# Seven block products for the gate projection of the last two token tiles

## The chip, the cores and the metric

The kernel runs on one core of a Trainium2 chip. The core has four engines that matter here and a queue engine. TensorE (PE) multiplies matrices into eight PSUM banks. VectorE (DVE) and ScalarE (ACT) can read PSUM and SBUF. GpSimd (POOL) reads and writes SBUF only. SyncE (SP) issues DMAs, and POOL issues DMAs as well. Each engine takes its instructions in the order in which they were written; an instruction that waits holds up everything behind it on its engine. The metric is the device time of one execution in microseconds (us).

## What is computed

A causal attention over 8 batches, 8 heads, 576 positions and a head size of 64, whose scores get a bias made of a running sum of `s`, is followed by a gated feed-forward block over its 4608 x 512 output `x`:

```python
g = x @ w_gate                                # 512 -> 1536
silu = g * (1.0 / (1.0 + np.exp(-g)))
val = x @ w_val                               # 512 -> 1536
out = (silu * val) @ w_out                    # 1536 -> 512
```

The change touches only the first two of these lines, and only for the last 1024 of the 4608 tokens.

## The kernel before, in words

**Tiles.** The feed-forward block goes over nine tiles of 512 tokens (`TT`, `NTT`), numbered 0 to 8. For a tile, `xt` is the transposed attention output: 128 partitions x 4 channel blocks x 512 tokens, bf16, in the ring `XT`. The 1536 inner features are twelve blocks of 128 (`ft`), taken in six pairs. `ffn_items(tt)` is the tile's work: `gate_value` (24 items), then `down_plain` (tiles 0 and 1) or `down_seven` (from tile 2, `FIRST7`). The main loop at the end takes these items one by one. After each it may issue a helper (loads, casts), and then `pump` issues as much attention work of later heads as is due. Attention lasts until tile 6; tiles 7 and 8 hold feed-forward work alone.

**Gate and value.** For each block `ft`, four matmuls of 512 columns make the gate product in a bank (L650, `wg`). ACT writes tanh(g/2) (L671, `th`). DVE makes (th + 1) * g (L673, `pp`). Four more matmuls make the value product (L650, `wv`), and DVE multiplies the two with a factor 0.5 (L684), which gives the block of `ht`. So silu comes out of tanh, whose table holds exp as well.

**Down projection.** `down_seven` already computes the product with `w_out` from seven block products instead of eight (Strassen's scheme). For that it needs, for each pair, sums of the `ht` blocks (`su`, two DVE instructions, L691 and L692) and differences that overwrite two blocks of `ht` (L693, on POOL, except the last pair's, which DVE makes). Its matmuls have 256 columns (L756). Its first 20 matmuls take the products of pairs 0 to 4 (`m3`, `m4`); then those of pair 5 follow; then `m1`, `m6`, `m5`, `m2`, `m7`. Between them ACT copies results from PSUM (L871 `s`, L805 `ysb`), DVE adds (L873, L795 into `de`; L815 into `ysb`), and POOL subtracts (L821). `m7` adds to a bank half that L795 has to have read first. POOL issues the stores of `ysb` (L828); in the last tile SP does.

**Banks.** `take()` hands out the PSUM bank that was given back longest ago, in the order of the code. A product that gets a bank waits until the last reader of its earlier contents has finished.

**Around it.** POOL also masks the attention weights (L388, L393), issues the DMAs of the attention output `xs` (L444), which SP transposes into `XT` (L451), and the small `kq` DMAs (L188). DVE copies transposed keys and queries (L288). `raw` holds loaded keys and queries, `KQ` their transposed forms, `VT` the values.

## Time and profile before

Three runs gave 373.15, 373.44 and 373.95 us, a median of 373.44 us. The profiled execution took 373.17 us, with a span of 371.5 us from its first to its last instruction.

| | busy us | share of the span |
|---|---|---|
| PE, matmuls | 361.1 | 97% |
| DVE | 289.9 | 78% |
| ACT | 241.2 | 65% |
| POOL | 219.6 | 59% |

| stage | first product at us | down projection from us | ends at us |
|---|---|---|---|
| tile 6 | 272.3 | 298.4 | 307.5 |
| tile 7 | 307.5 | 328.2 | 337.5 |
| tile 8 | 337.5 | 358.1 | 367 |

A profile row gives the line, the engine, the operation, the tile written and the tile read with their shapes, a count, the busy time and mean, and then the time that the engine was idle before such instructions and what ended it. Matmuls overlap in the records: a row says 379 ns for one of 512 columns, while the next starts about 216 ns later, so the pace of PE is read from start to start. In the timeline, instructions of a kind that follow each other are one line with the start of the first.

### The profile page before, as it was taken

How to read it: one execution, taken by the hardware profiler on the slowest of the kernel's cores; microseconds unless marked ns; L12 is line 12 of the kernel's file. 1: busy time of each engine (PE TensorE's matmuls, PEld its weight loads, DVE VectorE, ACT ScalarE, POOL GpSimd, SP SyncE). 2: the span in 40 equal slices, each digit the busy share in tenths (PEclk: the TensorE clock that was granted, in tenths of full speed). 3: DMA queues.
4: the chain of work that ended last, by engine and by line, in shares of the span. 5: the costliest groups of instructions: out<-in, count | busy, mean ns of one | idle time of the engine just before them, and what ended most of it. 6: DMA issues, size and time to landing. Idle time of an engine off the chain costs nothing.

```text
span 371.5 us, 8742 instructions
## 1 busy us (share of the span) xinstructions
PE 361.1 (97%) x3248; PEld 230.2 (62%) x3288; DVE 289.9 (78%) x583; ACT 241.2 (65%) x472; POOL 219.6 (59%) x334
## 2 busy tenths in 40 slices
PE   7899999999999999999999999999999999999995
PEld 6675556555555557755685568555865585476464
DVE  8878786288985999589967987689768867975984
ACT  8879776778886976687858875786466423323321
POOL 8996795945366556694749465965575506315320
PEclk9999999999999999999999999999999999999999
DMA  7999999899898985995689575995161113002003
GB/s 237 218 269 282 202 282 274 235 332 188 251 231 244 255 197 166 206 317 177 181 187 256 160 188 171 233 185 157 40 144 39 35 35 113 0 2 102 14 0 113
DMA packets 92301, 64.21 MB, mean 173 GB/s; under 512 B 72620, under 2 KB 78116, under 8 KB 92260
## 3 DMA queue, kind: packets, MB, share of 16 engines
q1 hardware_dynamic: 79188, 37.92, 42.9%
q0 software_dynamic: 13072, 25.75, 26.5%
q8 instruction: 25, 0.41, 0.5%
q14 instruction: 16, 0.13, 0.1%
HBM read 37.90 MB, written 19.86 MB: 155 GB/s over the span
## 4 chain that ended last, share of the span: by engine, by line
PE 89%; POOL 4%; DVE 3%; ACT 1%; issue 1%; DVEq 0%; POOLq 0%
PE banks L650 47%; PE banks L756 17%; PE banks L373 10%; PE banks L410 8%; PE banks L707 5%; POOL rawv L162 1%; DVE kq L330 1%; PE banks L301 1%; DVE ht L684 1%; ACT pt L383 1%; DVE pp L673 1%; PE banks L459 1%; DVE kq L288 0%; POOL cq L260 0%; POOL ck L260 0%
## 5 line engine op out<-in xcount | busy, mean ns | idle before, releaser
L383 ACT ACTIVATE pt<-banks 128x512 bf16<-128x512 f32 (+1 forms) x256 | 120.6, 510 | 28.8 <-PE banks L373 16.6
L650 PE MATMUL banks<-XT,wg 128*128 128x512 bf16 x418 | 110.3, 379 | 0.7
L650 PE MATMUL banks<-XT,wv 128*128 128x512 bf16 x412 | 109.3, 379 | 1.1
L671 ACT ACTIVATE th<-banks 128x512 bf16<-128x512 f32 x108 | 64.7, 599 | 54.8 <-PE banks L650 51.8
L673 DVE SCALAR_TENSOR_TENSOR pp<-th,banks 128x512 bf16<-128x512 bf16 x108 | 73.7, 682 | 19.5 <-ACT th L671 19.0
L684 DVE SCALAR_TENSOR_TENSOR ht<-pp,banks 128x512 bf16<-128x512 bf16 x108 | 74.2, 687 | 10.6 <-DVE pp L673 0.5
L373 PE MATMUL banks<-kq 128*128 128x128 bf16 (+4 forms) x576 | 76.2, 240 | 0.5 <-DVE kq L288 0.3
L693 POOL TENSOR_TENSOR ht<-ht 128x512 bf16<-128x512 bf16 x35 | 40.4, 1154 | 52.8 <-DVE su L691 52.7
L373 PEld LDWEIGHTS <-kq 128*128 128x128 bf16 x576 | 46.0, 98 | 30.2 <-issue 2.0
L650 PEld LDWEIGHTS <-wv 128*128 128x128 bf16 x432 | 38.4, 98 | 36.1 <-issue 0.2
L650 PEld LDWEIGHTS <-wg 128*128 128x128 bf16 x432 | 38.3, 98 | 33.6
L410 PEld LDWEIGHTS <-pt 128*128 128x128 bf16 x960 | 41.8, 98 | 17.4 <-issue 0.2
L388 POOL TENSOR_SCALAR_AFFINE_SELECT pt<-pt 128x512 bf16<-128x512 bf16 x56 | 36.5, 652 | 25.5 <-ACT pt L383 22.8
L410 PE MATMUL banks<-vt,pt 128*128 128x65 bf16 x960 | 46.8, 194 | 0.1
L444 POOL DMA_DIRECT2D xs<-ot x24 | 21.7, 903 | 29.2 <-DVE ot L427 28.6
L756 PEld LDWEIGHTS <-ht 128*128 128x128 bf16 x336 | 31.2, 98 | 4.3
L427 DVE TENSOR_TENSOR ot<-banks,rc 128x320 bf16<-128x320 f32 x64 | 31.5, 492 | 2.2
L188 POOL DMA_DIRECT2D kq<-HL x48 | 29.2, 610 | 0.5 <-issue 0.4
L756 PEld LDWEIGHTS <-su 128*128 128x128 bf16 x252 | 23.6, 98 | 3.3
L707 PE MATMUL banks<-wo,ht 128*128 128x512 bf16 x90 | 24.8, 379 | 0.3
L821 POOL TENSOR_TENSOR ysb<-ysb 128x512 f32<-128x512 f32 x12 | 15.3, 1272 | 15.3 <-DVE ysb L815 15.3
L756 PE MATMUL banks<-WS,ht 128*128 128x256 bf16 x168 | 22.9, 273 | 0.0
(101 smaller groups left out, 385.0 us busy)
## 6 DMA issues: line engine op xcount, KB each, us to landing
out_dram<-ysb POOLq DMA_DIRECT2D x32, 256.0 KB, 3.7
rawv<-in_v_dram SPq DMA_DIRECT2D x24, 256.0 KB
rawk<-in_k_dram SPq DMA_DIRECT2D x10, 576.0 KB
rawq<-in_q_dram SPq DMA_DIRECT2D x10, 576.0 KB
xs<-ot POOLq DMA_DIRECT2D x24, 160.0 KB, 3.4
ks<-ck SPq DMA_DIRECT2D x11, 288.0 KB
qs<-cq SPq DMA_DIRECT2D x11, 288.0 KB
rawk<-in_k_dram POOLq DMA_DIRECT2D x5, 576.0 KB, 6.6
```

Source lines behind the costliest of these rows:

```text
L373: nc.tensor.matmul(sc[:, o : o + w], T[:, 1, e * S + 128 * tj : e * S + 128 * (tj + 1)], T[:, 0, e * S + lo : e * S + hi], start=not maske ...
L383: nc.scalar.activation(pt[:, c0 : c0 + n], sc, AF.Exp, scale=0.125)
L388: nc.gpsimd.affine_select(pt[:, 1088:1600], pt[:, 1088:1600], pattern=[[0, 4], [1, 128]], compare_op=ALU.is_ge, fill=zreg, base=0, channel ...
L410: nc.tensor.matmul(av[:, bi * (D + 1) : (bi + 1) * (D + 1)], pt[:, c0 : c0 + 128], VT[b % 2][:, tj, h, :], start=(tj == 0), stop=(tj == bi),)
L427: nc.vector.tensor_mul(ot[:, :, e * D : (e + 1) * D], av3[:, :, 0:D], rc[:, :, None].to_broadcast([128, NCH, D]),)
L650: nc.tensor.matmul(view(bs, TT), w[:, c, f0 : f0 + 128], xt[:, c, :], start=(c == 0), stop=(c == 3),)
L671: nc.scalar.activation(th, pg, AF.Tanh, scale=0.5)
L673: nc.vector.scalar_tensor_tensor(pp, in0=th, scalar=1.0, in1=pg, op0=ALU.add, op1=ALU.mult)
L684: nc.vector.scalar_tensor_tensor(hp[:, 2 * k2 : 2 * k2 + 2, :].rearrange("p a n -> p (a n)"), in0=pp, scalar=0.5, in1=pv, op0=ALU.mult, op ...
L693: (nc.vector if ft == NFT - 1 else nc.gpsimd).tensor_sub(hp[:, 1:3, :], hp[:, 1:4:2, :], hp[:, 0:3:2, :])
L707: nc.tensor.matmul(view(pys[ts_], DM), hps[ft // 2][:, 2 * (ft % 2) + half, c0 : c0 + 128], WO[j][:, ft % WKO, :], start=(ft == 0), stop=( ...
L756: nc.tensor.matmul(ps, lhs(p), rhs(p), start=(first and p == 0), stop=(last and p == NP - 1), skip_group_check=True,)
```

## The change

**Gate by seven products.** In tile 7 for four of the six pairs, and in tile 8 for five, the gate product of a pair is split into blocks: two halves of the channels (k), two feature blocks (h), two halves of the tokens (t). Strassen's scheme makes the four results from seven products of two matmuls each, 256 columns wide: 14 matmuls in place of 8 of 512 columns. It needs five sums of the weight blocks (`gate_sum`, ten POOL instructions, each 768 or 512 elements a partition, into buffers of `raw` that are no longer in use) and five sums of the token blocks for each tile (`x_sum`, DVE, into `VT`). The products land in two banks, `bx` and `by`. The results are put together in fp32 in SBUF, in the place of `KQ`.

**The steps of a pair.** They are letters in the word lists `GATE7`, followed by the pair's or block's number:

- `A` makes the products 3, 4 (into `bx`), 6, 1 (into `by`); ACT copies `bx` to `S2`; POOL adds its halves into `D3`.
- `M`: DVE adds product 1 to that sum.
- `B` makes products 5, 2 and 7; ACT copies `bx` (two finished results) to `G4`; POOL subtracts it from `D3` (512 elements, fp32); ACT applies Silu to the two finished results.
- `R`: DVE adds `by` to `D3`, which gives the other two results; ACT applies Silu to them.
- `G` is a plain gate block with Silu straight from PSUM; `V` a value product; `H` DVE's multiplication of a block; `U` the two sums and the difference of a finished pair; `X` a sum of token blocks.

The words are issued in the order of the list, each engine keeping its own part of it.

**Silu.** In these two tiles the ScalarE function is Silu, so the multiplication that followed tanh (L673) is gone. A Silu of one element in tile 6, after the last exp, brings its table in; no other table is loaded after it.

**Hooks and stores.** The weight sums are issued at items 8, 12, ... 32 of tile 5 and 4, 8, 12 of tile 6. Two token sums of tile 7 are issued in tile 6's down projection, and the five of tile 8 in tile 7's. The stores of tiles 6 and 7 are issued by SP, not POOL.

```diff
--- before.py
+++ after.py
@@ -696,6 +696,170 @@
                     sus.append(su)
                 yield 1.0
 
+        GATE7 = {
+            NTT - 2: (
+                "G0 V0 X1 X0 X4 H0 G1 A1 V1 H1 M1 A2 U0 B1 V2 M2 "
+                "A3 R1 M3 V3 H2 B2 V4 H3 A4 R2 U1 M4 V5 H4 B3 V6 H5 "
+                "G10 R3 U2 V7 H6 B4 V8 H7 G11 R4 U3 H8 V9 H9 V10 U4 H10 V11 H11 U5"
+            ),
+            NTT - 1: (
+                "A0 M0 V0 A1 M1 B0 V1 A2 R0 H0 M2 B1 V2 H1 "
+                "A3 R1 U0 M3 V3 H2 B2 V4 H3 A4 R2 U1 M4 V5 H4 B3 V6 H5 "
+                "G10 R3 U2 V7 H6 B4 V8 H7 G11 R4 U3 H8 V9 H9 V10 U4 H10 V11 H11 U5"
+            ),
+        }
+        QT = TT // 2
+        gsum = {}
+        kqf = [
+            [t.rearrange("p a n -> p (a n)").bitcast(FP32) for t in row] for row in KQ
+        ]
+        G4 = [kqf[0][i][:, 0:1024].rearrange("p (a n) -> p a n", a=4) for i in range(2)]
+        D3 = [
+            kqf[1][i // 2][:, i % 2 * 512 : i % 2 * 512 + 512].rearrange("p (a n) -> p a n", a=2)
+            for i in range(3)
+        ]
+        S2 = kqf[1][1][:, 512:1024].rearrange("p (a n) -> p a n", a=2)
+
+        def gate_sum(i, j):
+            if i not in gsum:
+                tag = "raw" + "kkkqq"[i]
+                rawg = raw.tile([128, NR, J, D], FP32, tag=tag, name=tag)
+                gsum[i] = rawg.rearrange("p r j d -> p (r j d)").bitcast(BF16)[
+                    :, 0:1536
+                ].rearrange("p (j c a f) -> p j c a f", j=2, c=2, a=3)
+            n = 3 - j
+            w = WG[j].rearrange("p (k c) (a h f) -> p k h c a f", k=2, a=3, h=2)
+            dst = gsum[i][:, j, :, 0:n, :]
+            (k0, h0), (k1, h1), op = (
+                ((0, 0), (1, 1), ALU.add), ((0, 1), (1, 1), ALU.add), ((0, 0), (1, 0), ALU.add),
+                ((0, 1), (0, 0), ALU.subtract), ((1, 0), (1, 1), ALU.subtract),
+            )[i]
+            nc.gpsimd.tensor_tensor(
+                dst, w[:, k0, h0, :, 0:n, :], w[:, k1, h1, :, 0:n, :], op
+            )
+
+        def x_quarter(tt, k, t):
+            xt = XT[:, :, (tt % 3) * TT : (tt % 3 + 1) * TT]
+            return xt[:, 2 * k : 2 * k + 2, t * QT : (t + 1) * QT]
+
+        def x_sums(tt):
+            t = VT[tt % 2].rearrange("p c h e -> p (c h e)")
+            return t[:, 0 : 10 * QT].rearrange("p (s c n) -> p s c n", s=5, c=2)
+
+        def x_sum(tt, i):
+            (k0, t0), (k1, t1), op = (
+                ((0, 0), (1, 1), ALU.add), ((0, 1), (1, 1), ALU.subtract),
+                ((1, 0), (0, 0), ALU.subtract), ((0, 0), (0, 1), ALU.add),
+                ((1, 0), (1, 1), ALU.add),
+            )[i]
+            nc.vector.tensor_tensor(
+                x_sums(tt)[:, i], x_quarter(tt, k0, t0), x_quarter(tt, k1, t1), op
+            )
+
+        def gate_value_seven(tt, hps, sus):
+            xt = XT[:, :, (tt % 3) * TT : (tt % 3 + 1) * TT]
+            xs = x_sums(tt)
+            bx, by, sg, vb = {}, {}, {}, {}
+
+            def m(i, p, ps, start, stop):
+                j, a = divmod(p, 3)
+                for c in range(2):
+                    if i in (3, 4):
+                        k = i - 3
+                        lhs = WG[j][:, 2 * k + c, (2 * a + k) * 128 : (2 * a + k + 1) * 128]
+                    else:
+                        lhs = gsum[{1: 0, 2: 1, 5: 2, 6: 3, 7: 4}[i]][:, j, c, a, :]
+                    if i in (2, 5):
+                        rhs = x_quarter(tt, i // 5, i // 5)[:, c, :]
+                    else:
+                        rhs = xs[:, {1: 0, 3: 1, 4: 2, 6: 3, 7: 4}[i], c, :]
+                    nc.tensor.matmul(
+                        ps, lhs, rhs, start=(start and c == 0), stop=(stop and c == 1),
+                        skip_group_check=True,
+                    )
+
+            def halves(b):
+                return view(b, TT)[:, 0:QT], view(b, TT)[:, QT:TT]
+
+            def both(b):
+                return view(b, TT).rearrange("p (a n) -> p a n", a=2)
+
+            def open_pair(p):
+                bx[p] = take()
+                by[p] = take()
+                m(3, p, halves(bx[p])[0], True, False)
+                m(4, p, halves(bx[p])[1], False, False)
+                m(6, p, halves(by[p])[1], True, True)
+                m(1, p, halves(by[p])[0], False, False)
+                nc.scalar.copy(S2, both(bx[p]))
+                nc.gpsimd.tensor_add(D3[p % 3][:, 0], S2[:, 0], S2[:, 1])
+
+            def middle(p):
+                d = D3[p % 3]
+                nc.vector.tensor_add(d[:, 1], d[:, 0], halves(by[p])[0])
+
+            def close_pair(p):
+                m(5, p, halves(bx[p])[0], False, True)
+                m(2, p, halves(bx[p])[1], False, True)
+                m(7, p, halves(by[p])[0], False, True)
+                g = G4[p % 2]
+                pt = PTP[0].tile([128, PTW], BF16, tag="pt", bufs=PTP["bufs"], name="pt")
+                sg[p] = pt[:, 0 : 4 * QT].rearrange("p (a n) -> p a n", a=4)
+                nc.scalar.copy(g[:, 1:3], both(bx[p]))
+                give(bx[p])
+                nc.gpsimd.tensor_sub(D3[p % 3], D3[p % 3], g[:, 1:3])
+                nc.scalar.activation(sg[p][:, 1:3], g[:, 1:3], AF.Silu)
+
+            def result(p):
+                g = G4[p % 2]
+                nc.vector.tensor_add(g[:, 0:4:3], D3[p % 3], both(by[p]))
+                give(by[p])
+                nc.scalar.activation(sg[p][:, 0:4:3], g[:, 0:4:3], AF.Silu)
+
+            def plain(ft):
+                bs = products("g", ft, xt)
+                pp = hpool.tile([128, TT], BF16, tag="pp", name="pp")
+                nc.scalar.activation(pp, view(bs, TT), AF.Silu)
+                give(bs)
+                p, h = divmod(ft, 2)
+                sg[p, h] = pp
+
+            def value(ft):
+                vb[ft] = products("v", ft, xt)
+
+            def times(ft):
+                p, h = divmod(ft, 2)
+                if h == 0:
+                    hps.append(hpool.tile([128, 4, HT], BF16, tag="ht", bufs=NP, name="ht"))
+                left = (
+                    sg[p, h] if (p, h) in sg
+                    else sg[p][:, 2 * h : 2 * h + 2].rearrange("p a n -> p (a n)")
+                )
+                nc.vector.tensor_mul(
+                    hps[p][:, 2 * h : 2 * h + 2, :].rearrange("p a n -> p (a n)"),
+                    left, view(vb[ft], TT),
+                )
+                give(vb.pop(ft))
+
+            def sums(p):
+                hp = hps[p]
+                su = PTP[0].tile([128, 3, HT], BF16, tag="su", bufs=NP, name="su")
+                nc.vector.tensor_add(su[:, 0:2, :], hp[:, 0:2, :], hp[:, 2:4, :])
+                nc.vector.tensor_add(su[:, 2, :], hp[:, 0, :], hp[:, 3, :])
+                (nc.vector if p == NP - 1 else nc.gpsimd).tensor_sub(
+                    hp[:, 1:3, :], hp[:, 1:4:2, :], hp[:, 0:3:2, :]
+                )
+                sus.append(su)
+
+            does = {
+                "A": open_pair, "M": middle, "B": close_pair, "R": result, "G": plain,
+                "V": value, "H": times, "U": sums, "X": lambda i: x_sum(tt, i),
+            }
+            for word in GATE7[tt].split():
+                does[word[0]](int(word[1:]))
+                if word[0] in "GVAB":
+                    yield 1.0
+
         def down_plain(tt, hps):
             pys = {}
 
@@ -823,7 +987,7 @@
                     )
                 flush()
 
-                def store(eng=nc.sync if end else nc.gpsimd):
+                def store(eng=nc.sync if tt >= NTT - 3 else nc.gpsimd):
                     for i in range(2):
                         eng.dma_start(
                             out[a + i * HT : a + i * HT + 128, :],
@@ -891,7 +1055,7 @@
         def ffn_items(tt):
             hps, sus = [], []
             flush()
-            yield from gate_value(tt, hps, sus)
+            yield from (gate_value_seven if tt in GATE7 else gate_value)(tt, hps, sus)
             if tt < FIRST7:
                 yield from down_plain(tt, hps)
             else:
@@ -1067,6 +1231,17 @@
         at_item(17, w_load, "o", 1)
         at_item(21, load_one, 5, "k", (0, NR), nc.gpsimd)
         at_item(23, load_one, 5, "q", (0, NR), nc.gpsimd)
+        at_tile = {}
+        for i in range(10):
+            key = (NTT - 4, 8 + 4 * i) if i < 7 else (NTT - 3, 4 * i - 24)
+            at_tile[key] = [lambda i=i: gate_sum(*divmod(i, 2))]
+        at_tile[NTT - 3, 26] = [
+            lambda: nc.scalar.activation(warm, warm, AF.Silu),
+            lambda: x_sum(NTT - 2, 2),
+        ]
+        at_tile[NTT - 3, 28] = [lambda: x_sum(NTT - 2, 3)]
+        for i in range(5):
+            at_tile[NTT - 2, 24 + i] = [lambda i=i: x_sum(NTT - 1, i)]
         for tt in range(NTT):
             lo = H * (tt + 1) + LAGS[tt]
             hi = min(H * (tt + 2) + LAGS[tt + 1], BH + 2)
@@ -1089,7 +1264,7 @@
                     do_later(1)
                 if seconds:
                     seconds.pop(0)()
-                for f in hook.pop(n, ()):
+                for f in hook.pop(n, ()) if tt == 0 else at_tile.get((tt, i), ()):
                     f()
                 done = min(1.0, max(0, n - n0) / (span - n0))
                 if tt == 0:
```

## The prediction

> **What bounds the kernel now.** I read the page first, then busy times by stage, then the rows of tile 7's gate stage by form, then timelines at the joints. Of the page, the engines and the chain that ended last:
>
> ```profile
> PE 361.1 (97%) x3248; PEld 230.2 (62%) x3288; DVE 289.9 (78%) x583; ACT 241.2 (65%) x472; POOL 219.6 (59%) x334
> ...
> PE 89%; POOL 4%; DVE 3%; ACT 1%; issue 1%; DVEq 0%; POOLq 0%
> ```
>
> PE is the bound. The gate stages of tiles 7 and 8 (each engine's busy us, then clock and DMA):
>
> ```profile
> 307.50:328.20 20.70, 20.59 (x96) 9.39 (x97) 17.98 (x33) 7.37 (x13) 9.56 (x11) 1.00 0.14 51
> 337.50:358.10 20.60, 20.49 (x95) 9.32 (x96) 17.99 (x33) 7.26 (x13) 9.78 (x11) 1.00 0.14 52
> ```
>
> PE never waits, DVE is nearly full, ACT and POOL have more than half free. The rows of tile 7's stage that give prices:
>
> ```profile
> L684 DVE SCALAR_TENSOR_TENSOR ht<-pp,banks 128x512 bf16<-128x512 bf16 x11 | 7.6, 688 | 1.3
> L673 DVE SCALAR_TENSOR_TENSOR pp<-th,banks 128x512 bf16<-128x512 bf16 x11 | 7.5, 682 | 1.0 <-ACT th L671 1.0
> L671 ACT ACTIVATE th<-banks 128x512 bf16<-128x512 f32 x12 | 7.2, 597 | 13.3 <-PE banks L650 12.2 <-DVE pp L673 1.1
> L693 POOL TENSOR_TENSOR ht<-ht 128x512 bf16<-128x512 bf16 x5 | 5.8, 1151 | 10.3 <-DVE su L691 10.3
> L821 POOL TENSOR_TENSOR ysb<-ysb 128x512 f32<-128x512 f32 x2 | 2.5, 1263 | 5.0 <-DVE ysb L815 5.0
> L691 DVE TENSOR_TENSOR su<-ht 128x512 bf16<-128x512 bf16 x5 | 2.1, 424 | 0.2
> L692 DVE TENSOR_TENSOR su<-ht 128x256 bf16<-128x256 bf16 x5 | 1.4, 285 | 0.0
> L815 DVE TENSOR_TENSOR ysb<-de,banks 128x512 f32<-128x512 f32 x1 | 0.7, 689 | 1.3 <-PE banks L756 1.3
> L805 ACT COPY ysb<-banks 128x512 f32<-128x512 f32 x1 | 0.6, 585 | 1.4 <-PE banks L756 1.4
> ```
>
> See that POOL is slow at elementwise work: 1.15 us for what DVE does in 0.42. And the timeline at tile 8's handover to the down projection:
>
> ```profile
> 358.14 2.78 PE L756 MATMUL banks<-wo,ht 128*128 128x256 bf16 x24
> ...
> 360.21 0.42 DVE L693 TENSOR_TENSOR ht<-ht 128x512 bf16<-128x512 bf16 x1
> ...
> 360.76 0.82 PE L756 MATMUL banks<-WS,su 128*128 128x256 bf16 x6
> ```
>
> DVE finishes the last pair 2.5 us after PE's last value product (358.14 to 360.63). The 24 matmuls of m3 and m4 cover exactly that; there is no further cover. From a tile's first gate product to m1 it is 23.34 us (307.53 to 330.87).
>
> **What PE saves.** Eight 512-column matmuls start 1.726 us apart (309.26 to 310.99); 84 of 256 columns take 9.17 us, 0.109 each, weight loads hidden. A pair falls from 1.726 to 14 x 0.109 = 1.529: 0.197 saved, and 1.77 us over nine pairs. That is the whole gain, and it stands only if nothing else holds PE.
>
> **What a pair costs elsewhere.**
> - DVE: the two L673 (1.36) go. M is 0.42 (as L795), R 0.69 (as L815), two H stay at 0.69. 3.45 becomes 3.19 with U.
> - ACT: two copies (0.585) and two Silu (0.60, as tanh; the trace has no Silu, and 512-element ACT rows of several functions lie at 0.59 to 0.60): 2.37 of 3.25 us. Not a bound.
> - POOL: one U difference before (1.15); now also the 256-element fp32 addition and the 512-element fp32 subtraction. The subtraction is L821's shape: 1.27; its lower bound is a one-input POOL operation of that width (L388, 0.65), and I take 1.27, since type and inputs agree. The addition lies between 0.24 (L393) and 1.27, taken as 0.70; it hides beside R. Together 3.12 us a pair, against PE's 3.25 (1.53 gate, 1.73 value).
>
> **The loop.** POOL is full, and it also waits. On POOL, `U1` stands between the subtractions of pairs 2 and 3; on DVE, `U1` stands behind `R2`, and `R2` waits for the subtraction of pair 2. So from one subtraction to the next: 1.27 + 0.10 (POOL to DVE; not shown, between ACT to DVE 0.04 and DVE to POOL 0.15) + 0.61 (R; an independent DVE instruction starts 0.08 before the recorded end) + 0.42 (U's first sum) + 0.15 (DVE to POOL, 306.51 to 306.66) + 1.09 (POOL's U, start to start) = 3.64 us. PE's pair takes 3.25. The other loop, through ACT (R, Silu, then the copy of the next pair), is 1.27 + 0.10 + 0.69 + 0.09 + 0.60 + 0.585 + 0.07 = 3.40: also longer.
>
> **Tile 7, written down queue by queue** (us from its first product, each instruction in code order at its row's time). Five pieces of G and V, and A1, A2 and B1 follow without a wait. POOL does the additions of pairs 1 and 2 (to 6.3), then U0 (to 7.5). The subtraction of pair 1 starts at 7.45, those of 2, 3, 4 at 10.86, 14.49, 18.12. R4 ends at 20.18. Behind it DVE has U3, H8, H9, U4, H10, H11: 3.87 us, to 24.05. PE by its own work would be through at 19.92 and at m1 at 22.55. Now m4 of pair 5 waits for H11, and m1 starts at 24.44: 1.10 later than the 23.34 of before. A bank wait of 0.65 at A4 (H2 still reads) lies inside that.
>
> **Tile 8.** It starts with a seven-product pair, and POOL's last L821 of tile 7 ends 2.35 us into it (as before: 309.88 - 307.53), ahead of the first addition. Subtractions start at 4.40, 7.81, 11.44, 15.07, 18.70. H11 ends at 24.6, m1 starts at 25.0: 1.66 late.
>
> **Other edits.**
> - Token sums: 0.42 each (L691). Tile 7's first three fit before A1's later products. Of tile 8's five, four stand ahead of L873 in tile 7's down projection, which begins late; L795 then ends about 28.6, m7 is due at 28.37: 0.25 us, bounds 0 and 0.7.
> - Weight sums on POOL: 1.15 (512) and 1.64 (768; scaled with the 0.18 that L388 and L393 leave as fixed). In tile 5 one of 1.15 comes behind the `kq` DMAs and ahead of the select at 262.35; that then ends 263.75, and PE's matmuls that need it were at 263.18: 0.65. The other selects have 0.6 to 2 us in hand. Bounds 0 and 2.0 (below).
> - The table load (L204, 1.28 us and 0.20 for the element): ACT idles 2.94 before L871 at 300.96. Nothing; without that cover 1.5.
> - Stores to SP: behind SP's last transpose (304.25) nothing waits; POOL sheds 2.18 us after 309.82. Nothing; were SP late, stores would still have a tile's time.
>
> One row speaks against the weight sums: DVE's copies of L288 next to POOL's selects.
>
> ```profile
> 246.29 0.46 DVE L288 COPY kq<-pk 64x1152 bf16<-64x1152 bf16 x1
> ...
> 263.52 0.93 DVE L288 COPY kq<-pk 64x1152 bf16<-64x1152 bf16 x1
> ```
> ```profile
> 263.47 0.65 POOL L388 TENSOR_SCALAR_AFFINE_SELECT pt<-pt 128x512 bf16<-128x512 bf16 x1
> ```
>
> The second copy lasted until POOL's instruction was over. Two copies (246.29 and 250.88) will meet a sum and may wait about 1.0 each; DVE idles 7.3 of the 39 us there, so I take nothing, with 2.0 as the upper end. The Trainium skill, "SBUF — State Buffer", section "SBUF: two separate sides", says that VectorE and GpSimd lock a shared port pair for whole instructions, when VectorE runs in a two-port mode or reads two SBUF inputs. By that rule every such copy waits out the sum, and the total would be up to 2.0 us above mine; by the rows of the uncrowded copies (0.46) it would be mine.
>
> **The sum**, on the profiled execution's 373.17 us (span 371.5 and 1.67 around it; 0.27 below the median): 373.17 + 0.65 + 1.10 + 0.25 + 1.66 = 376.83. PE's saving is inside the two tile terms.
>
> **The rivals.**
> - *POOL keeps up, and PE stays the bound* (faster). Place: the subtraction. It decides if the loop falls below 3.25, so if the subtraction takes 0.88 or less. For it: the lower bound of 0.65. Against it: L821 is the same type, shape and number of inputs. The last subtraction could then start when B4's copy is there (16.47 in tile 7, 16.27 in tile 8), and m1 would start at 22.79 and 22.59: 373.17 - 0.55 - 0.75 = 371.9, or 372.5 with the 0.65.
> - *Half way.* Waits and lags eat about the saving: 372.7 to 374.2.
> - *Longer lags.* Each hand-over 0.15, and no DVE instruction starts before the recorded end of the last: the loop is 3.81. The same list then gives m1 at 25.25 and 26.0 and 0.7 at m7: 373.17 + 0.65 + 1.9 + 0.7 + 2.7 = 379.1.
> - *The clock drops while PE waits.* PE's waits would add up to 1.9 and 2.7 us in the two tiles. Against it: around PE's wait of 0.64 us at 14.0 the granted clock read 1.00, as in every 5 us of the first 40; the trace has no longer wait between matmuls. If 3.4 us after each tile's wait ran at half speed, 1.7 a tile is added: 376.8 + 3.4 = 380.2. The Trainium skill, "TensorE: Matmul & The Clock Gate", section "What's actually happening", says that the array falls to half its clock after an idle window of about 3.4 us; by that rule waits as short as these don't do it.
>
> That the products pace slower than counted I exclude: the 0.109 is measured with fresh weights each time.
>
> **How the numbers follow.** Forecast (374.2 to 378.2) 0.60, longer lags 0.12, clock 0.03, half way 0.10, POOL keeps up 0.15. A measurement of this kernel tells apart about 0.2%, 0.75 us. Faster 0.15, same 0.10, slower 0.75. The predicted time is 376.8. The range leaves out the clock's case and most of the fast one: 372.6 to 379.2.
>
> **What would show it.** POOL over 85% busy in both gate stages, its subtraction near 1.27 us and 3.6 us from one to the next; R waiting for POOL; PE waits at m3, m4 or A for DVE's multiplications, about 1.9 us in tile 7 and 2.7 in tile 8 in all; products of A and B 0.109 apart; one wait near 263. I am wrong if the subtraction takes under 0.9 us, or if the tail from R4 to H11 is much shorter than 3.9 us.

## The result, and the profile after

The changed kernel took 381.90 us (median of six runs, 380.9 to 383.87), against 373.29 us before (six runs on the same chip): a ratio of 1.0228, with a 95% interval of 1.0204 to 1.0251. It is slower, as forecast, but by 8.6 us where 3.7 were forecast, and 2.7 us beyond the upper end of the range. The profiled execution took 383.87 us, with a span of 382.1.

The page of the changed kernel, engines and the chain that ended last:

```profile
PE 366.6 (96%) x3342; PEld 236.3 (62%) x3342; DVE 292.2 (76%) x587; ACT 252.4 (66%) x492; POOL 246.0 (64%) x354
...
PE 62%; DVE 14%; POOL 9%; DMA 6%; issue 5%; ACT 2%; DVEq 0%; POOLq 0%; ACTq 0%
```

PE's own work is not the story: it was 89% of the chain and is 62% now, and DVE, POOL and loads have taken the difference. To place the loss, I compare the starts of landmarks in the two traces: DVE's 64 instructions that write the attention output (L427 in both), and then the first `m1` matmul of tiles 6, 7 and 8.

| stretch | lag behind before at its end, us | added in it, us |
|---|---|---|
| start, and tiles 0 to 4 (code that is the same) | 2.73 | 2.73 |
| tile 5, gate stage | 4.52 | 1.79 |
| tile 5, handover to the down projection | 8.94 | 4.42 |
| tile 6 | 8.95 | 0.01 |
| `m1` of tile 6 to `m1` of tile 7 | 9.85 | 0.90 |
| `m1` of tile 7 to `m1` of tile 8 | 11.05 | 1.20 |

The first row is not the change's. In that execution some DMAs landed late, at the start and again between 89 and 119 us; all eleven kernels below run that code, and the profiles of nine show 0.0 to 0.3 there, those of two 2.6 and 3.1. It is a matter of single executions. (At the other end, from tile 8's `m1` to the end of the span, before takes 0.4 us more than the changed kernel.) What is left is 6.2 us in tile 5 and 2.1 us in tiles 7 and 8. The forecast had 0.65 and 3.0 for these two.

The line numbers shift with the code: in the changed kernel the weight sums are L737, the matmuls of the down projection L920 and those of the seven products L776; in the kernels made from before the first two are L714 and L775.

**Tile 5's handover.** Before, at this place:

```profile
262.52 0.43 DVE L691 TENSOR_TENSOR su<-ht 128x512 bf16<-128x512 bf16 x1
262.54 0.92 POOL L444 DMA_DIRECT2D xs<-ot  x1
...
262.87 0.28 DVE L692 TENSOR_TENSOR su<-ht 128x256 bf16<-128x256 bf16 x1
```

The timeline of the changed kernel, DVE and POOL with PE's wait:

```profile
266.88 1.16 POOL L737 TENSOR_TENSOR rawk<-wg 128x512 bf16<-128x512 bf16 x1
...
267.04 2.16 DVE L691 TENSOR_TENSOR su<-ht 128x512 bf16<-128x512 bf16 x1
...
267.99 0.24 POOL L393 TENSOR_SCALAR_AFFINE_SELECT pt<-pt 128x64 bf16<-128x64 bf16 x1
268.18 0.92 POOL L444 DMA_DIRECT2D xs<-ot  x1
...
268.29 0.27 PE L410 MATMUL banks<-vt,pt 128*128 128x65 bf16 x3 [0.59 <-POOL pt L393]
...
269.11 0.65 POOL L388 TENSOR_SCALAR_AFFINE_SELECT pt<-pt 128x512 bf16<-128x512 bf16 x1
269.12 2.39 DVE L692 TENSOR_TENSOR su<-ht 128x256 bf16<-128x256 bf16 x1
269.71 1.64 POOL L737 TENSOR_TENSOR rawk<-wg 128x768 bf16<-128x768 bf16 x1
271.30 0.31 POOL L393 TENSOR_SCALAR_AFFINE_SELECT pt<-pt 128x64 bf16<-128x64 bf16 x1
...
271.57 0.28 PE L920 MATMUL banks<-WS,su 128*128 128x256 bf16 x1 [2.03 <-DVE su L692]
```

The two sums of the last pair (L691, L692) take 0.43 and 0.28 us at this place before. Here they take 2.16 and 2.39. No wait for a semaphore is listed before them: they start, and end only after several of POOL's instructions. The first ends at 269.20, when the weight sum, the select and the issue of a DMA are over (269.10); the second then starts 0.01 us after POOL's next, and ends at 271.51, 0.16 us after the weight sum behind that one (271.35) and beside a select. The issue alone need not do it: before, both sums ran beside the same issue in their usual time. `m1` needs their result, so PE stands for 2.03 us. The select's wait of 0.59 just before is the one wait that was forecast (0.65).

**Tiles 7 and 8.** Their groups by form (from 310 us on), whose counts are nine for the nine pairs. Here `kq` stands for `S2`, `G4` and `D3`, which lie in its place; L810 is the subtraction, L795 the addition, L815 R and L811 a Silu:

```profile
L810 POOL TENSOR_TENSOR kq<-kq,kq 128x512 f32<-128x512 f32 x9 | 11.4, 1268 | 2.2 <-ACT kq L808 2.2
...
L795 POOL TENSOR_TENSOR kq<-kq 128x256 f32<-128x256 f32 x9 | 6.7, 742 | 3.5 <-ACT kq L794 3.5
L815 DVE TENSOR_TENSOR kq<-kq,banks 128x512 f32<-128x512 f32 x9 | 6.2, 688 | 7.8 <-POOL kq L810 7.8
L811 ACT ACTIVATE pt<-kq 128x512 bf16<-128x512 f32 x9 | 5.7, 630 | 0.3
```

and POOL's timeline in tile 7:

```profile
327.34 1.27 POOL L810 TENSOR_TENSOR kq<-kq,kq 128x512 f32<-128x512 f32 x1 [1.25 <-ACT kq L808]
...
330.92 1.27 POOL L810 TENSOR_TENSOR kq<-kq,kq 128x512 f32<-128x512 f32 x1
333.39 1.15 POOL L849 TENSOR_TENSOR ht<-ht 128x512 bf16<-128x512 bf16 x1 [1.20 <-DVE su L847]
334.51 1.26 POOL L810 TENSOR_TENSOR kq<-kq,kq 128x512 f32<-128x512 f32 x1
```

The subtraction takes 1.268 us and starts 3.58 and 3.59 us apart (forecast: 1.27, 3.64). PE's listed waits in tile 7 and at its `m1`:

```profile
327.56 0.38 PE L776 MATMUL banks<-vt,rawq 128*128 128x256 bf16 x2 [0.48 <-DVE ht L838]
337.93 2.14 PE L920 MATMUL banks<-wo,ht 128*128 128x256 bf16 x17 [0.26 <-DVE ht L838]
340.38 0.50 PE L920 MATMUL banks<-wo,ht 128*128 128x256 bf16 x3 [0.32 <-DVE ht L838]
340.72 0.82 PE L920 MATMUL banks<-WS,su 128*128 128x256 bf16 x6
```

(L838 is H.) They stand at A4's bank, at `m3`/`m4` and just ahead of `m1`, as the prediction's list has it. A listed wait is short of the loss: from start to start PE loses 1.7 us in tile 7 and 2.2 in tile 8 (forecast 1.9 and 2.7), the 0.90 and 1.20 and the saving of the seven products that they eat. From the tile's first product it is 24.24 us to `m1` (forecast 24.44), and 24.54 in tile 8 (forecast 25.0).

### The profile page after: what moved, and what is told of

Its sections match the earlier page's. It is cut to its first block, busy times and chain, and to the rows that moved or that the text cites. A ratio compares the mean times of both kernels' runs of the same rounds, so it can differ in the third digit from the quotient of the medians.

```text
span 382.1 us, 8955 instructions
## 1 busy us (share of the span) xinstructions
PE 366.6 (96%) x3342; PEld 236.3 (62%) x3342; DVE 292.2 (76%) x587; ACT 252.4 (66%) x492; POOL 246.0 (64%) x354
## 4 chain that ended last, share of the span: by engine, by line
PE 62%; DVE 14%; POOL 9%; DMA 6%; issue 5%; ACT 2%; DVEq 0%; POOLq 0%; ACTq 0%
PE banks L650 28%; PE banks L920 15%; PE banks L373 8%; PE banks L410 6%; PE banks L871 3%; POOL kq L810 3%; DVE pp L673 2%; DVE ht L684 2%; DVE kq L330 2%; DMA rawk<-in_k_dram 2%; DMA XT<-xs 2%; DVE kq L288 1%; DVE ht L838 1%; DMA xs<-ot 1%; DMA pk<-ks 1%
## 5 line engine op out<-in xcount | busy, mean ns | idle before, releaser
L650 PE MATMUL banks<-XT,wg 128*128 128x512 bf16 x360 | 93.1, 379 | 0.3 <-DMA XT<-xs 0.2
L673 DVE SCALAR_TENSOR_TENSOR pp<-th,banks 128x512 bf16<-128x512 bf16 x84 | 57.3, 682 | 18.1 <-ACT th L671 17.7
L671 ACT ACTIVATE th<-banks 128x512 bf16<-128x512 f32 x84 | 50.4, 600 | 29.9 <-PE banks L650 29.2
L684 DVE SCALAR_TENSOR_TENSOR ht<-pp,banks 128x512 bf16<-128x512 bf16 x84 | 57.6, 686 | 7.8 <-DVE pp L673 0.5
L693 POOL TENSOR_TENSOR ht<-ht 128x512 bf16<-128x512 bf16 x25 | 28.9, 1156 | 30.6 <-DVE su L691 30.5
L650 PEld LDWEIGHTS <-wg 128*128 128x128 bf16 x360 | 31.4, 98 | 25.6 <-issue 0.2
L920 PEld LDWEIGHTS <-ht 128*128 128x128 bf16 x336 | 31.0, 99 | 7.5 <-DVE ht L838 3.0
L427 DVE TENSOR_TENSOR ot<-banks,rc 128x320 bf16<-128x320 f32 x64 | 31.5, 492 | 2.2
L920 PEld LDWEIGHTS <-su 128*128 128x128 bf16 x252 | 23.8, 99 | 5.9 <-DVE su L692 2.3
L871 PE MATMUL banks<-wo,ht 128*128 128x512 bf16 x96 | 25.8, 380 | 0.0
L1035 ACT COPY s<-banks 128x256 f32<-128x256 f32 x14 | 5.2, 372 | 30.5 <-DVE de L1037 17.9
L920 PE MATMUL banks<-wo,ht 128*128 128x256 bf16 x168 | 22.4, 273 | 1.4 <-DVE ht L838 1.4
```

The lines of the kernel that those rows point to most:

```text
L427: nc.vector.tensor_mul(ot[:, :, e * D : (e + 1) * D], av3[:, :, 0:D], rc[:, :, None].to_broadcast([128, NCH, D]),)
L650: nc.tensor.matmul(view(bs, TT), w[:, c, f0 : f0 + 128], xt[:, c, :], start=(c == 0), stop=(c == 3),)
L671: nc.scalar.activation(th, pg, AF.Tanh, scale=0.5)
L673: nc.vector.scalar_tensor_tensor(pp, in0=th, scalar=1.0, in1=pg, op0=ALU.add, op1=ALU.mult)
L684: nc.vector.scalar_tensor_tensor(hp[:, 2 * k2 : 2 * k2 + 2, :].rearrange("p a n -> p (a n)"), in0=pp, scalar=0.5, in1=pv, op0=ALU.mult, op ...
L871: nc.tensor.matmul(view(pys[ts_], DM), hps[ft // 2][:, 2 * (ft % 2) + half, c0 : c0 + 128], WO[j][:, ft % WKO, :], start=(ft == 0), stop=( ...
```

## The experiments

Two theories of the loss in tile 5 stood at first. **L**: POOL's weight sums hold out DVE's two-input sums and its copies; the loss depends on where the sums fall. **N**: the sums are near to free, and the loss comes with the rest of the change (Silu, the moved stores, the longer program). For tiles 7 and 8 the theory was the prediction's: the loop over POOL's subtraction is longer than PE's pair, and its lag outgrows the cover at the handover.

The times of before differ a little between the chips that the groups of runs had (medians 373.37 for the first four runs, 373.64 for the next four, 373.86 and 373.67 for the last), so each ratio is against its own.

### The weight sums alone

Before, with the ten weight sums on POOL where the change has them; their results are not used, and gate, value and down projection are computed as before.

```diff
+        for i in range(10):
+            key = (NTT - 4, 8 + 4 * i) if i < 7 else (NTT - 3, 4 * i - 24)
+            at_tile[key] = [lambda i=i: gate_sum(*divmod(i, 2))]
```

> The kernel before, with only the ten weight sums added on POOL at the change's places; their results are not used, so the gate is computed as before. Theory L (in tile 5 a weight sum on POOL and a DVE instruction with SBUF inputs shut each other out for whole instructions; PE then waits and its clock drops): 4 to 7 us above before, 377.5 to 380.5, with DVE rows of L691, L692 or L288 of 1 us and more in tile 5 and a clock below 1.00 there. Rival N (tile 5's long DVE rows are an accident of one execution, and the sums cost only the wait of the late select): 0.3 to 1 us above before.

It took 378.97 us (378.72 to 379.17), ratio 1.0126 (1.0085 to 1.0167): 5.6 us more. The lag of the attention output is 0.03 up to tile 4, then 0.98, 1.86, and from the handover on 5.85. The part of the expectation on the clock did not come: it stayed at 1.00 in tile 5. The handover's timeline:

```profile
264.22 1.17 POOL L714 TENSOR_TENSOR rawk<-wg 128x512 bf16<-128x512 bf16 x1
264.37 2.16 DVE L691 TENSOR_TENSOR su<-ht 128x512 bf16<-128x512 bf16 x1
...
266.45 2.40 DVE L692 TENSOR_TENSOR su<-ht 128x256 bf16<-128x256 bf16 x1
267.05 1.64 POOL L714 TENSOR_TENSOR rawk<-wg 128x768 bf16<-128x768 bf16 x1
...
268.91 0.28 PE L775 MATMUL banks<-WS,su 128*128 128x256 bf16 x1 [2.03 <-DVE su L692]
```

It is the picture of the changed kernel to 0.01 us. The first two steps (0.95 and 0.89) are two copies of L288 that meet a sum, at 246.31 and 251.86: they take 1.41 and 1.33 us in place of 0.46. At PE's first attention product behind the wait (269.03, 264.42 before) the lag is 4.61; the rest, to 5.85, comes behind DVE, which has one more held copy to make (1.30 us at 269.25), so that PE waits 0.48 us for the attention output at 272.29. So the sums alone cost 5.6 us, and N falls.

### No sums at the handover

The same, without the three sums after items 24, 28 and 32 of tile 5 (again unused).

```diff
-        for i in range(10):
+        for i in (0, 1, 2, 3, 7, 8, 9):
```

> The kernel before with seven of the ten unused weight sums on POOL: the three that come after items 24, 28 and 32 of tile 5, around the start of its down projection, are left out. Theory L says that these three hold the last pair's sums (L691, L692) that m1 waits for: in the run with all ten sums the lag behind before rose there by 4.0 of 5.6 us. Expected 1.3 to 2.3 us above before, 374.7 to 375.7. If the cost goes with the number of sums, it is 0.7 of 5.6: 3.9 us above.

375.65 us (375.42 to 377.71), ratio 1.0053 (1.0025 to 1.008): 2.0 us over before. The three sums that were left out made 3.6 of the 5.6 (3.2 by the lags of the two traces); by count, three of ten would have been 1.7. The place decides. What is left in the trace is the two copies (lag 1.86) and one more step of 0.8. That step is at the handover too, for one sum still falls there: the one after item 20, which POOL reaches only behind four `kq` DMAs.

```profile
264.23 1.17 POOL L714 TENSOR_TENSOR rawk<-wg 128x512 bf16<-128x512 bf16 x1
...
264.38 1.31 DVE L691 TENSOR_TENSOR su<-ht 128x512 bf16<-128x512 bf16 x1
...
265.33 0.45 POOL L393 TENSOR_SCALAR_AFFINE_SELECT pt<-pt 128x64 bf16<-128x64 bf16 x1
...
265.84 0.27 PE L410 MATMUL banks<-vt,pt 128*128 128x65 bf16 x3 [0.80 <-POOL pt L393]
```

It makes the select late, as the prediction had it (0.65). And L691 met the same sum and the same select as in the run before, but this time its hold ended 0.29 us after the sum, and the select took 0.45 us in place of 0.25. So a hold can end between two of POOL's instructions or last over several; what decides it, no run here shows.

### The weight sums on VectorE, same places

The changed kernel with one engine changed.

```diff
-            nc.gpsimd.tensor_tensor(
+            nc.vector.tensor_tensor(
                 dst, w[:, k0, h0, :, 0:n, :], w[:, k1, h1, :, 0:n, :], op
```

> The changed kernel with the ten weight sums issued on DVE instead of POOL, at the same places. Theory L: what tile 5 lost comes back, 374.5 to 376.5; PE's clock stays at 1.00 in tile 5; what is left above before is the two late handovers of tiles 7 and 8 (0.9 and 1.2 us in the changed kernel's trace). Rival N: within 1 us of the changed kernel, 381 to 383.

377.59 us (377.42 to 382.17), ratio 1.012 (1.0069 to 1.0172). The direction is L's, 4.3 us less than the change, but the value is 1.1 above the range expected. The sums take 0.68 to 0.79 us on DVE (the means of their four groups by shape and buffer), and in tile 5's gate stage, where DVE has no room, each pushes PE: the lag grows in steps of about half a us to 2.2. I had not counted that.

### All weight sums in tile 6

The changed kernel, with the sums on POOL after items 2, 4, ... 20 of tile 6.

```diff
-            key = (NTT - 4, 8 + 4 * i) if i < 7 else (NTT - 3, 4 * i - 24)
+            key = (NTT - 3, 2 * i + 2)
```

> The changed kernel with the ten weight sums on POOL after items 2, 4, ... 20 of tile 6, where DVE makes no copies of keys and queries and the down projection has not begun. Theory L: most of tile 5's loss comes back, with some held pair sums (L691) in tile 6 that PE's work covers: 375 to 378. Rival N: 381 to 383.

380.18 us (379.43 to 380.67), ratio 1.0157 (1.0114 to 1.0199): a miss by 2.2 us. I had taken tile 6 for safe because no handover lies there. Its timeline shows that every pair has the same two sums:

```profile
283.35 2.32 DVE L691 TENSOR_TENSOR su<-ht 128x512 bf16<-128x512 bf16 x1
283.73 1.65 POOL L737 TENSOR_TENSOR rawk<-wg 128x768 bf16<-128x768 bf16 x1
...
297.39 0.36 PE L410 MATMUL banks<-vt,pt 128*128 128x65 bf16 x6 [1.41 <-POOL pt L388]
298.05 2.47 DVE L691 TENSOR_TENSOR su<-ht 128x512 bf16<-128x512 bf16 x1
```

The attention output is 4.3 us later at the end of tile 6 than at its start. So the cost is not one unlucky place: each pair of a gate stage has sums to hold, and selects behind a weight sum are late as well (PE's 1.41 us above).

### No seven-product pair

The changed kernel with all pairs of tiles 7 and 8 plain and no weight or token sums; Silu and the stores on SP stay.

```diff
-        GATE7 = {...}
+        PLAIN = " ".join(
+            f"G{f} V{f} H{f}" + (f" U{f // 2}" if f % 2 else "") for f in range(NFT)
+        )
+        GATE7 = {NTT - 2: PLAIN, NTT - 1: PLAIN}
```

> The changed kernel with every pair of tiles 7 and 8 a plain one: no weight sums, no token sums, no seven products; Silu, the freed DVE multiplication and the stores on SP stay. Both theories: PE stays the bound, so within 0.7 us of before, 372.8 to 374.0. If part of the loss ahead of tile 5 (2.75 us in the changed kernel's trace) belongs to the longer program itself, it shows here as 1 to 2.7 us above before.

373.53 us (372.93 to 376.87), ratio 0.9998 (0.9965 to 1.0031), and `m1` to `m1` 29.89 us in both tiles, as before. The lag ahead of tile 5 is 0.05 us, so the longer program costs nothing there either. Silu and the moved stores cost nothing that shows, and gain nothing either, though DVE lost twelve multiplications a tile: PE was the bound there.

### The sums where DVE has room

The changed kernel with the sums on DVE in the down projections of tiles 5 and 6. By the windows of before, DVE is busy for 3.19 of 5 us there (265 to 270), against 9.36 of 10 in the stage ahead.

```diff
-            key = (NTT - 4, 8 + 4 * i) if i < 7 else (NTT - 3, 4 * i - 24)
+            key = (NTT - 4, 31 + i) if i < 6 else (NTT - 3, 25 + i)
...
-            nc.gpsimd.tensor_tensor(
+            nc.vector.tensor_tensor(
```

> The changed kernel with the weight sums on DVE, at items 31 to 36 of tile 5 and 31 to 34 of tile 6, where DVE has idle time in the down projection. Theory L: the 2.2 us that the sums on DVE still cost in the gate stages nearly go, and what is left is the two late handovers: 1.8 to 2.8 us above before, 375.2 to 376.2. Rival: DVE's sums cost as much there as in the gate stage, 377 to 378.

375.86 us (375.2 to 377.9), ratio 1.0058 (1.0032 to 1.0084). The lag grows by 0.02 in tiles 5 and 6: the ten sums are free there, though one of them was held to 2.29 us (at 273.84, beside POOL's select and subtraction), with nobody waiting. `m1` to `m1` is 30.81 and 31.41 us, 2.4 over before in sum, so all that is left lies in tiles 7 and 8. That is their loss by itself.

### The pair sums ahead of R

To shorten the loop over the subtraction, the pair sums U were put ahead of R.

```diff
-"... A4 R2 U1 M4 V5 ... G10 R3 U2 V7 ... G11 R4 U3 H8 ..."
+"... A4 U1 R2 M4 V5 ... G10 U2 R3 V7 ... G11 U3 R4 H8 ..."
```

> As the run before it, with U of a pair put ahead of R of the next one in both word lists (DVE order, and so POOL's). Loop theory (subtraction, R, U's first sum on DVE, U on POOL: 3.6 us a pair against PE's 3.25 makes the handovers late): the loop falls to the other one, 3.4 us, and each handover comes 0.4 to 0.8 us earlier: 0.7 to 1.6 us less than the run before it. If the tail from R4 to H11 alone makes the handover late: within 0.4 us of the run before it.

378.71 us (377.46 to 380.59), ratio 1.0115 (1.0075 to 1.0155): `m1` to `m1` is 31.79 and 32.65 us, about 1 us worse a tile, not better. Its timeline says why:

```profile
325.66 1.27 POOL L810 TENSOR_TENSOR kq<-kq,kq 128x512 f32<-128x512 f32 x1 [0.86 <-ACT kq L808]
...
326.40 0.81 DVE L847 TENSOR_TENSOR su<-ht 128x512 bf16<-128x512 bf16 x1
327.14 0.28 DVE L848 TENSOR_TENSOR su<-ht 128x256 bf16<-128x256 bf16 x1
327.34 0.67 DVE L815 TENSOR_TENSOR kq<-kq,banks 128x512 f32<-128x512 f32 x1
```

U (L847) now comes while the subtraction runs, and is held until that ends (its mean is 0.61 us, 0.42 in the changed kernel); R (L815) could have started at 327.0 and starts behind U. In the order of the change, R waits for the subtraction, so U stands where POOL is idle (but for the first pair's, whose L848 took 0.81 us beside POOL's addition at 322.35). R itself reads one input from PSUM and is not held: in the changed kernel it took 0.69 us at 325.43, beside POOL's addition at 325.36. The subtractions start up to 4.17 us apart here (349.98 to 354.15), where 3.40 was expected and 3.58 was the change's pace: the loop grew, and `m1` came later with it. That it could be cut in this way was wrong, and for the same reason as tile 5.

### Fewer pairs

If the lag of the loop has to outgrow a cover before it costs, few pairs in a row should keep PE's saving. Five pairs: 1 and 2 in tile 7, 0 to 2 in tile 8, and plain ones behind them, with five weight sums on DVE in tile 5's down projection.

```diff
+            NTT - 2: (
+                "G0 V0 X1 X0 X4 H0 G1 A1 V1 H1 M1 A2 U0 B1 V2 M2 "
+                "G6 R1 V3 H2 B2 G7 H3 U1 V4 V5 R2 H4 H5 G8 V6 U2 H6 V7 H7 "
+                "G9 U3 V8 H8 G10 V9 H9 U4 V10 H10 G11 V11 H11 U5"
+            ),
+            NTT - 1: (
+                "A0 M0 V0 A1 M1 B0 V1 A2 R0 H0 M2 B1 V2 H1 "
...
```

> Five seven-product pairs in place of nine (pairs 1 and 2 of tile 7, pairs 0 to 2 of tile 8), so that the last three pairs of each tile are plain and give POOL and DVE time to catch up; five weight sums of 768 elements are left, on DVE at items 32 to 36 of tile 5. If the slack of the plain pairs absorbs the loop, PE is the bound again and saves 5 x 0.197 = 1.0 us, less 0.2 to 0.6 for what the sums delay: 372.4 to 373.0. If the handover stays late: 373.5 to 374.5.

372.99 us (372.38 to 376.34), ratio 0.9983 (0.9956 to 1.0009), which is not told apart from no change. `m1` to `m1` is 29.52 and 29.73 us: tile 7 keeps its whole saving (0.37 of 2 x 0.197), tile 8 keeps 0.16 of 0.59. Tile 8 starts with a seven-product pair, and PE waits there for M (L799), 0.27 us as listed and 0.43 from start to start.

So the next kernel has tile 7's order in both tiles, four pairs in all.

```diff
+        TWO = (
+            "H0 G1 A1 V1 H1 M1 A2 U0 B1 V2 M2 "
+            "G6 R1 V3 H2 B2 G7 H3 U1 V4 V5 R2 H4 H5 G8 V6 U2 H6 V7 H7 "
+            "G9 U3 V8 H8 G10 V9 H9 U4 V10 H10 G11 V11 H11 U5"
+        )
+        GATE7 = {NTT - 2: "G0 V0 X1 X0 X4 " + TWO, NTT - 1: "G0 V0 " + TWO}
```

In this and the next expectation "theory L" stands for the account of tiles 7 and 8, as their brackets say.

> Two pairs (1 and 2) in each of the two tiles, four in all, with tile 7's order in both, so that no pair stands first in a tile; the other pairs are plain. The five wide weight sums stand on VectorE in tile 5's down projection. Theory L (the loop over GpSimd's subtraction costs PE nothing until its lag has eaten the cover at m3/m4): PE's four savings of 0.197 stay whole, m1 to m1 is 29.50 in both tiles against 29.89, no PE wait for VectorE in the gate stages, total 0.8 less than before: 372.5 to 373.0. Rival (each seven-product pair costs a net 0.23, as 2.1 us over nine pairs would have it): 0.9 more than before, 374.1 to 374.7.

372.20 us (372.1 to 374.93), ratio 0.996 (0.9935 to 0.9986): 0.4% faster than before, with an interval clear of 1. The time lies 0.3 us below the expected range, and 1.7 us below the median of before; the landmarks, which leave out the start and the end, give the smaller gain. Its first `m1` matmuls:

```profile
301.09 0.82 PE L914 MATMUL banks<-WS,su 128*128 128x256 bf16 x6
...
330.61 0.82 PE L914 MATMUL banks<-WS,su 128*128 128x256 bf16 x6
...
360.14 0.82 PE L914 MATMUL banks<-WS,su 128*128 128x256 bf16 x6
```

29.52 and 29.53 us, against 29.89 before: 0.73 of the 0.79 us that four pairs save PE. A fixed price for each pair is out.

Three pairs in a row, six in all (five narrow weight sums more, in tile 6's down projection):

```diff
+        THREE = (
+            "H0 G1 A1 V1 H1 M1 A2 U0 B1 V2 M2 A3 R1 M3 V3 H2 B2 V4 H3 "
+            "G8 R2 U1 V5 H4 B3 V6 H5 G9 R3 U2 V7 H6 V8 H7 G10 U3 H8 V9 H9 "
+            "G11 U4 V10 H10 V11 H11 U5"
+        )
```

> Three pairs (1, 2, 3) in each tile, six in all; pairs 0, 4 and 5 plain. Five wide weight sums on VectorE in tile 5's down projection, five narrow ones in tile 6's. Theory L: two steps of the loop of 3.64 us against PE's 3.25 leave VectorE about 0.8 us late, and each plain pair behind them needs 2.0 of VectorE's 3.45 us and gives 1.4 back, so that the handover finds it in time: m1 to m1 29.30 in both tiles, total 1.2 less than before, 372.1 to 372.6. Rival (a net cost of 0.23 a pair): 1.4 more, 374.6 to 375.2.

372.83 us (372.09 to 375.73), ratio 0.998 (0.9953 to 1.0006), and 29.54 us in both tiles (expected 29.30): two pairs more saved nothing. PE's timeline has no wait that is listed, but one step is too long:

```profile
316.81 1.03 PE L650 MATMUL banks<-XT,wv 128*128 128x512 bf16 x4
317.67 1.03 PE L650 MATMUL banks<-XT,wg 128*128 128x512 bf16 x4
318.76 1.02 PE L650 MATMUL banks<-XT,wv 128*128 128x512 bf16 x4
319.62 0.60 PE L770 MATMUL banks<-XT,rawk 128*128 128x256 bf16 x4
```

Four matmuls take 0.86 us from start to start (316.81 to 317.67), but from G8 to V5 it is 1.09. V5 gets the bank that the multiplication H2 reads until 318.70. If that is the cause, six products of B3 ahead of V5 cover it:

```diff
-"G8 R2 U1 V5 H4 B3 V6 H5 G9 ..."
+"G8 R2 U1 B3 V5 H4 V6 H5 G9 ..."
```

> The kernel with three pairs a tile, with the products B3 moved ahead of the value product V5 in both lists. If the 0.22 us that TensorE lost per tile there (from the start of G8's matmuls to V5's 1.09 us, against 0.86 elsewhere) is V5's wait for the bank that the multiplication H2 still reads, 0.65 us of B3 cover it: m1 to m1 29.31 in both tiles against 29.54, total 0.46 less than with V5 first. If the loss has another cause, m1 to m1 stays at 29.54.

372.02 us (371.85 to 374.92), ratio 0.995 (0.9922 to 0.9979). PE's timeline at the same place, and its `m1` rows:

```profile
317.63 1.03 PE L650 MATMUL banks<-XT,wg 128*128 128x512 bf16 x4
318.49 0.60 PE L770 MATMUL banks<-XT,rawk 128*128 128x256 bf16 x4
```
```profile
301.08 0.82 PE L914 MATMUL banks<-WS,su 128*128 128x256 bf16 x6
...
330.40 0.82 PE L914 MATMUL banks<-WS,su 128*128 128x256 bf16 x6
...
359.73 0.82 PE L914 MATMUL banks<-WS,su 128*128 128x256 bf16 x6
```

0.86 again, and 29.32 and 29.33 us (expected 29.31): 1.13 of the 1.18 us that six pairs save. The trace of the kernel with V5 first agrees: V5's first matmul starts at 318.76, 0.06 us behind the end of H2. The bank was the cause. The total is 0.8 us less than with V5 first, not 0.46, but the two ran on different chips. It is the fastest of those tried; between four and six pairs the times alone do not decide, the landmarks do.

## Why the prediction was right and wrong

| term of the sum | forecast | measured |
|---|---|---|
| early copies beside weight sums | 0 (upper end 2.0) | 1.86 (sums alone) |
| tile 5's handover | 0.65 (one select) | 3.99 (sums alone); 0.75 with the one sum at 264.23 |
| tile 7 | 1.10 | 0.90 |
| tile 8, with `m7` of tile 7 | 1.91 | 1.20 |

Added to 373.29, the measured terms give 373.29 + 1.86 + 3.99 + 0.90 + 1.20 = 381.2, against a lowest run of 380.9 and a median of 381.9.

**What held.** PE's saving of 0.197 a pair: 0.73 for four pairs and 1.13 for six where nothing else was in the way. The prices of nearly all new instructions: subtraction 1.268 (1.27), addition 0.742 (0.70), Silu 0.63 and 0.59 (0.60), M 0.415 (0.42), R 0.688 (0.69). The loop: 3.58 (3.64). The late select: 0.75 (0.65) where no other sum stood at the handover. In tile 7 the tail from R4 to H11 took 3.84 us (336.49 to 340.33; forecast 3.87). So of the rivals "POOL keeps up" was out, and "longer lags" too.

**What was too large.** Tile 8's term: 1.20 for 1.91. From that tile's first product the subtractions started at 4.35, 7.56, 11.14, 14.73 and 18.32 us; the list had the first at 4.40 and the last at 18.70, with steps of 3.41 and 3.63 for 3.21 and 3.58. And four token sums in a row took 1.43 us, 0.36 each, not 0.42, so that `m7`'s 0.25 did not show. POOL's share was wrong as well: 13.09 of 20.5 us in tile 7 (64%) and 15.02 of 20.7 in tile 8 (73%), not over 85%. The 3.12 of 3.64 us hold for a pair between pairs, and a stage also has ends and a plain pair.

**What failed** is the step on the weight sums, "so I take nothing, with 2.0 as the upper end". It failed twice. First, the size for one copy was right ("may wait about 1.0 each"; 0.95 and 0.87 in the kernel with the sums alone), but DVE's idle time did not take it up: PE's attention products waited 0.59 and 0.58 us for the output behind the copy. Idle time in the mean is no cover for an instruction with someone waiting. Second, I looked at the copies of L288 alone. The rule that I cited, from the Trainium skill, "SBUF — State Buffer", section "SBUF: two separate sides", names VectorE instructions with two SBUF inputs too, and that is what L691 and L692 are. Two of them stand at the handover, right ahead of `m1`. By the rule I had written "up to 2.0 us above mine"; applied to all the instructions that it names, it leads to the handover. The trace agrees with it that they are held, with 2.16 us for 0.43 and 2.39 for 0.28; one whole instruction, as the rule has it, is what the 1.31 us at 264.38 shows, while these two lasted over more. Rows of before already showed a copy of 0.93 beside a select. Of the 3.99 us, 3.24 went when the three sums behind the forecast one were left out.

**The clock.** The rival of a slower clock happened, almost without a price, and not where it was expected: from 310 to 372, over tiles 7 and 8, the granted clock read 1.00. The windows of the changed kernel around the wait, clock in the third column from the right:

```profile
269.00:272.00 3.00, 0.97 (x11) 0.65 (x10) 2.97 (x4) 0.18 (x1) 2.99 (x5) 1.00 0.24 55
272.00:276.00 4.00, 4.00 (x25) 2.78 (x23) 3.41 (x7) 0.68 (x2) 0.89 (x1) 0.57 0.17 37
```

After PE's idle 2.03 us the granted clock was 0.57 for four us. In the kernel with the sums alone the same wait of 2.03 us was followed by 1.00:

```profile
265.00:270.00 5.00, 2.37 (x25) 1.91 (x25) 4.97 (x4) 0.37 (x1) 4.99 (x7) 1.00 0.22 51
270.00:275.00 5.00, 4.24 (x50) 3.42 (x49) 3.59 (x10) 2.23 (x6) 1.17 (x4) 1.00 0.08 14
```

The two executions lose 6.21 and 5.83 us in tile 5, so by this comparison the clock made about 0.4 at most. DVE's backlog held PE in those us anyway, or so I read it; no run took the clock alone. Over the six runs, too, the mean granted clock does not go with the time: the two runs at 1.00 took 380.9 and 383.46. The Trainium skill, "TensorE: Matmul & The Clock Gate", section "What's actually happening", has the drop behind an idle window of about 3.4 us in a window that runs freely. The longest listed wait here is 2.03, so "waits as short as these don't do it", as I had it by that rule, does not hold; that the same wait did it in one execution and not in another would fit the free-running window, but in neither was PE idle for a whole one. What set it off stays open.

## What to carry to other kernels

Before work is moved to GpSimd because it is idle, list what VectorE runs at the same time with two SBUF inputs or as a bf16 copy: such an instruction can be held for one GpSimd instruction or for several in a row, and it costs where someone waits for its result, whatever the mean idle time says. Put such sums where VectorE has room and do them there. A scheme that saves PE a little per block, and takes a longer loop through slow engines, pays for a few blocks with plain ones behind them; look at every cover that the lag can eat, PSUM banks included, not only at the handover.

## What the runs showed of the hardware

- The hold can last over several GpSimd instructions that follow each other without a gap: L691, with two inputs in SBUF, ended after a sum, a select and a DMA issue (2.16 us for 0.43), in the changed kernel and with the sums alone. It need not: at 264.38, without the later sums, it ended 0.29 us after the sum (1.31), and the select was late instead. Beside a DMA issue alone it took 0.43 before, while L693 on VectorE took 0.85 beside one at 184.76 (0.42 at 263.07).
- VectorE instructions with one input in PSUM were not held: R took 0.69 us in the mean of nine, as at 325.43 beside POOL's addition. This fits the loop in tiles 7 and 8, which ran at its forecast pace beside a busy GpSimd.
- The granted clock can fall after 2.03 us of listed idle time of PE (0.57 over the next four us), and need not.
- A wait of 0.22 us of PE did not appear in the listed waits, and one of 0.43 was listed as 0.27; the loss is seen from start to start.
